# State products in two runs of three units, with output pieces on both sides, in an attention block followed by a gated feed-forward layer

## The chip, the cores and the metric

The kernel runs on one core of a Trainium2 chip. The metric is the device time of one execution in microseconds (us), lower is better. A time is the median of several executions of the same program.

## What is computed

There are 8 batches of 8 heads; each has 512 tokens `x` and 32 state rows, 64 wide. Tokens attend to the state and the state attends to the tokens ("recurrent read"), both through the same scores:

```
xread = softmax(scale * x @ state^T) @ state        # 512 rows a head and batch
sread = softmax(scale * state @ x^T) @ x            #  32 rows a head and batch
y     = heads of [xread; sread] side by side        # (8 * 544) x 512
out   = (relu(y @ w_gate) * (y @ w_val)) @ w_out    # 512 -> 1536 -> 512
```

The kernel never forms `xread`. It multiplies the state with the two weights first, `U = state @ w` (the **state products**), so that `xread @ w` becomes attention weights times `U`. For the 32 state rows a batch it forms `sread` itself.

## The kernel before

**Stages.** The work of a batch is cut into 12 slots, one for each 128 columns of the 1536 hidden features. A slot `(b, jf)` holds four matmuls of `gv` (gate and value, line 314), a ReLU of the gate on ScalarE (`relu`, L338), the product with the value on VectorE (`mult`, L342) and one **output piece** (`out_piece`, four matmuls at L351 with `w_out`) for a tile of hidden features made 18 slots earlier (`lag`). Every third piece closes an output tile: `fin_x` copies it out on ScalarE (L359) and SyncE sends it to memory.

**Order.** The schedule is written out by hand. A literal program covers batches 0 and 1 and the start of batch 2; from slot (2, 4) on a loop emits one slot after the other, and the dictionary `units` adds extra work at the end of a slot (`at(b, jf, f, ...)`). Each engine runs its instructions in the order in which the code emits them.

**Extra work in the loop.** For batch `b` (3 to 7) the slots of batch `b - 1` carry: two halves of the scores with their softmax (`att_half`: matmuls L198, exponential on ScalarE L205, sum, reciprocal and scaling on VectorE L211, L213, L217), the state products (`u_block`), the recurrent read (`sr`) and the transposition of its result (`sr_T`). Slot (2, 10) also holds `state_prep`, which transposes the state of batches 4 to 7 on TensorE (L127) and copies it out on ScalarE (L131).

A **unit** of state products (`u_unit`, L289) is eight matmuls of tile size 64 rows by 32 columns, which share the array, and fills two PSUM banks; `u_out` (L299) casts each bank into `U`. There are six units a batch: gate and value for three stretches of 512 columns. `u_block` emits two units:

```
def u_block(b, lo, engs=("act", "act", "dve", "dve")):
    for w in range(2):
        u_unit(b, w, lo)
        for kc in range(NK):
            u_out(b, w, lo, kc, engs[2 * w + kc])
```

so ScalarE casts both banks of the first unit and VectorE both banks of the second. The blocks stand in slots 7, 9 and 11.

`sr_mm` (L262) is 32 matmuls with 32 columns of weights each; `sr_norm` on VectorE (L269, L271) writes the tile `sn`; `sr_T` (L275) is one TensorE transposition of `sn`, copied into `br` on ScalarE (L276). `x_pad` (L254, GpSimd) fills the other operand of `sr_mm`, two batches ahead in the same buffer, so it waits for the `sr_mm` that used that buffer last. `x_next` (L140, GpSimd) casts the tokens of the next batch.

**Banks.** Of eight PSUM banks six rotate (`"r"`): each request takes the next in turn, whoever asks. `gv` takes two, a unit two, a half of the scores one, `sr_mm` one, `sr_T` one, `state_T` one. The other two (`"o"`) alternate as output accumulators. A matmul into a bank waits until the last reader of that bank is done.

Of the kernel before, what the change touches and what calls it, by code (L numbers as in the profile page):

```python
# [16 lines left out]
def kernel(  # L17
# [17 lines left out]
    NF = d_ff // 128  # L35
# [19 lines left out]
    NK = 2  # L55
# [7 lines left out]
    NX, DP = 2, 66  # L63
# [15 lines left out]
    given, turn = [], {"r": 0, "o": 0}  # L79

    def bank(name, kind="r"):

        if given:
            n = given.pop(0)
        else:
            n = turn["r"] % 6 if kind == "r" else 6 + turn["o"] % 2
            turn[kind] += 1
        return psum.tile([128, 512], FP32, name=name, tag=f"b{n}")

    held = {}  # L90
# [33 lines left out]
    def state_T(g):  # L124
        ps = held["st", g] = bank("stT_ps").bitcast(BF16)[:, 0:512]
        for i in range(4):
            nc.tensor.transpose(ps.rearrange("p (q i m) -> p q i m", i=4, m=8)[:, :, i],  # L127
                                st_b[:, g % 3, i].rearrange("p h d -> p (h d)"), id128)
# [31 lines left out]
    def x_T(b, j):  # L160

        if b not in xT:
            xT_alloc(b)
        ps = bank("xT_ps").bitcast(BF16)[:, 0:512].rearrange("p (c t) -> p c t", c=NC)
        for c in range(NC):
            if b == 0 and j < 2:
                nc.tensor.transpose(ps[:, c], x_head(b)[:, c, 2 * j:2 * j + 2].rearrange("p h d -> p (h d)"), id128)
            else:
                v, h = (x_tail(b), 2 * j - HK) if b == 0 else (xb[b], 2 * j)
                for h2 in range(2):  # L170
                    nc.tensor.transpose(ps[64 * h2:64 * h2 + 64, c], v[:, c, h + h2], id128)
        held["xT", b, j] = ps
# [4 lines left out]
    def x_T2(b, half):  # L177
        if b not in xT:
            xT_alloc(b)
        ps = held["xT2", b, half] = bank("xT_ps").bitcast(BF16).rearrange("p (c j t) -> p c j t", c=NC, j=2)  # L180
        for j in range(2):
            for c in range(NC):
                for h2 in range(2):
                    nc.tensor.transpose(ps[64 * h2:64 * h2 + 64, c, j], xb[b][:, c, 4 * half + 2 * j + h2], id128)
# [68 lines left out]
            src = src.rearrange("p c h d -> p h c d")  # L253
            nc.gpsimd.tensor_copy(out=v[:, hs:hs + src.shape[1]], in_=src)  # L254

    def sr_mm(b):

        ps = held["sr", b] = bank("sr_ps")[:, 0:2 * DP].rearrange("p (r d) -> p r d", r=2)
        for c in range(NC):
            for parity in range(2):  # L260
                for j in range(NJ):
                    nc.tensor.matmul(ps[32 * j:32 * j + 32, parity, 0:D + 1], e_sn[b][:, parity, c, 32 * j:32 * j + 32],  # L262
                                     xa[:, b % NX, H * c + 2 * j + parity, 0:D + 1],
                                     start=(c == 0 and parity == 0), stop=(c == NC - 1), skip_group_check=True)

    def sr_norm(b):
        ps = held["sr", b]
        rr = small.tile([128, 2], FP32, name="rr", tag="rr")
        nc.vector.reciprocal(out=rr, in_=ps[:, :, D])  # L269
        sn = held["sn", b] = small.tile([128, 2, D], BF16, name="sn", tag="sn")  # L270
        nc.vector.tensor_tensor(out=sn, in0=ps[:, :, 0:D], in1=rr.to_broadcast([128, 2, D]), op=ALU.mult)  # L271
# [20 lines left out]
    def u_unit(b, w, lo):  # L292

        u_alloc(b)
        ps = held["u", b, w, lo] = [bank("up"), bank("up")]
        u_mm(ps, b, w, lo, 512)

    def u_out(b, w, lo, kc, eng):
        copy[eng](out=U[b][:, w, kc, lo:lo + 512], in_=held["u", b, w, lo][kc])  # L299
# [17 lines left out]
    def gv(b, jf):  # L317
        if b not in hsb:
            hsb[b] = hpool.tile([128, NF, S], BF16, name="h_sb", tag="h_sb")
        held["gv", b, jf] = [bank("gv_ps"), bank("gv_ps")], hsb[b][:, jf], S  # L320
        for w in range(2):
            for kc in range(NK):
                gv_mm(held["gv", b, jf][0], b, jf, w, kc)

    def gvs(jf):
        f0 = jf * 128
        ps = [bank("gv_ps"), bank("gv_ps")]
        nt = B * Ns
        for w, wsb in ((0, wg_sb), (1, wv_sb)):
            for j in range(NJ):  # L330
                nc.tensor.matmul(ps[w][:, 0:nt], wsb[:, j, f0:f0 + 128], br[:, j].rearrange("p b n -> p (b n)"),  # L331
                                 start=(j == 0), stop=(j == NJ - 1))
        held["gv", B, jf] = ps, hs_sb[:, jf], nt

    def relu(b, jf):
        ps, dst, n = held["gv", b, jf]
        g_sb = held["g", b, jf] = gpool.tile([128, 512], BF16, name="g_sb", tag="g_sb")
        nc.scalar.activation(out=g_sb[:, 0:n], in_=ps[0][:, 0:n], func=AF.Relu)  # L338

    def mult(b, jf):  # L340
        ps, dst, n = held["gv", b, jf]
        nc.vector.tensor_tensor(out=dst, in0=ps[1][:, 0:n], in1=held["g", b, jf][:, 0:n], op=ALU.mult)  # L342
# [4 lines left out]
    def out_mms(src, b, tsub, jfs):  # L347
        if jfs[0] == 0:
            held["o", b, tsub] = o_bank()
        for jf in jfs:  # L350
            nc.tensor.matmul(held["o", b, tsub], src[:, jf, tsub * 128:(tsub + 1) * 128], wo_sb[:, jf],  # L351
                             start=(jf == 0), stop=(jf == NF - 1))
# [4 lines left out]
    def fin_x(b, tsub, eng="act"):  # L357
        o_sb = opool.tile([128, d_model], FP32, name="o_sb", tag="o_sb")
        copy[eng](out=o_sb, in_=held["o", b, tsub])  # L359
        nc.sync.dma_start(out=out_rows(b, tsub), in_=o_sb)  # L360

    def fin_s(t2):
        outr = out.rearrange("(b s) m -> b s m", s=SP)
        o_sb = opool.tile([128, d_model], FP32, name="o_sb", tag="o_sb")
        nc.scalar.copy(out=o_sb, in_=held["o", B, t2])
        for bq in range(4):
            eng = nc.sync if bq % 2 == 0 else nc.scalar
            eng.dma_start(out=outr[t2 * 4 + bq, S:SP], in_=o_sb[bq * Ns:(bq + 1) * Ns])
# [14 lines left out]
    def out_part(b, i):  # L383
        tsub, q = divmod(i, 3)
        out_mms(hsb[b], b, tsub, list(range(4 * q, 4 * q + 4)))

    def out_piece(b, i):
        out_part(b, i)
        if i % 3 == 2:
            fin_x(b, i // 3)  # L390
# [37 lines left out]
    def spin(n, cols=512):  # L428
        for i in range(n):
# [6 lines left out]
             "sc": att_sc, "ex": att_exp, "nr": att_sum, "nx": att_scale, "aT2": att_T2, "ao2": att_out2, "aT": att_T, "ao": att_out,  # L436
             "c": c_unit, "co": c_out, "u": u_unit, "uo": u_out, "gv": gv, "re": relu, "mu": mult, "o": out_part,
             "of": fin_x, "xn": x_next, "xp": x_pad, "sr": sr_mm, "sn": sr_norm}
    program = """
    dx.1.0.2 dx.1.1.2 stc.0.0.act stc.0.1.dve spin.7 stT.0@0 xc.0.0.dve dw.0.0.128 sto.0.act dw.1.0.128 on xc.0.1.dve  # L440
# [31 lines left out]
        assert not given  # L472


    units = {}

    def at(b, jf, f, *args):
        units.setdefault(NF * b + jf, []).append(lambda: f(*args))

    def u_block(b, lo, engs=("act", "act", "dve", "dve")):  # L480
        for w in range(2):
            u_unit(b, w, lo)
            for kc in range(NK):
                u_out(b, w, lo, kc, engs[2 * w + kc])

    def att_half(b, kc):
        att_up(b, kc)
# [7 lines left out]
        att_scale(b, kc)  # L495

    def sr(b):
        sr_mm(b)
        sr_norm(b)

    def state_prep(lo, hi):
# [4 lines left out]
    first, lag = 2 * NF + 4, 18  # L506
    at(2, 4, x_dma, 4, (nc.sync,))
    at(2, 10, state_prep, 4, B)
    for b in range(3, B):
        s, late = b - 1, 2 if b == 3 else 0  # L510
        for i, jf in enumerate((3, 5)):
            at(s, jf + late, att_half, b, i)
        for i, jf in enumerate((7, 9, 11)):
            at(s, jf, u_block, b, 512 * i)
        if b + 1 < B:
            at(s, 9, x_next, b + 1)
            at(s, 9, x_pad, b + 1)
        if b + 2 < B:
            at(s, 10, x_dma, b + 2, (nc.sync,))
    for b in range(B):  # L520
        s, jf = {0: (2, 2), 1: (2, 3), 2: (2, 8), 3: (2, 11)}.get(b, (b - 1, 9))
        if b > 1:
            at(s, jf, sr, b)
        at(*divmod(NF * s + jf + 2, NF), sr_T, b, "act")
    for g in range(first, NF * (B + 1)):
        b, jf = divmod(g, NF)
        gv(b, jf) if b < B else gvs(jf)
        relu(b, jf)
        mult(b, jf)
        if g >= lag:  # L530
            out_piece(*divmod(g - lag, NF))
        for f in units.get(g, ()):
            f()
    for t2 in range(2):
        out_mms(hs_sb, B, t2, list(range(NF)))
        fin_s(t2)
# [33 lines left out]
```

The softmax here doesn't subtract the row's maximum and nothing guards it: scores larger than these inputs give would overflow.

## Time and profile before

| | |
|---|---|
| median of 13 runs | 226.47 us (226.0 to 227.14) |
| profiled execution: time / span | 227.01 us / 225.2 us |
| TensorE busy | 217.8 us (97%) |
| VectorE busy | 129.0 us (57%) |
| ScalarE busy | 124.9 us (55%) |
| GpSimd busy | 53.4 us (24%) |
| granted TensorE clock | full in every slice |

PE is TensorE's matmuls, PEld its weight loads, DVE VectorE, ACT ScalarE, POOL GpSimd, SP SyncE; L289 is line 289 of the kernel. A timeline line reads: start in us, length in us, engine, line, operation, result<-operands, shape and count, and in brackets the idle time before it with what ended it. Lengths of pipelined matmuls overlap: what a group cost TensorE is the distance from its start to the next start. A step of four wide matmuls takes 0.86 us in this measure.

### The profile page before, as it was taken

The page shows a single profiled execution, that of the slowest core. Times are in us where ns is not written, and L with a number is a line of the kernel's source. Part 1 is how long each engine was busy: PE and PEld are TensorE (multiplying, and loading weights), DVE is VectorE, ACT ScalarE, POOL GpSimd, SP SyncE. Part 2 cuts the span into 40 slices and gives each one's busy share as a digit, 9 for nine tenths or more (in the row PEclk, how much of TensorE's full clock was granted, in tenths as well). Part 3 has the DMA queues.
Part 4 walks back from the last instruction along what each step waited for, and adds up shares of the span by engine and source line. Part 5 has one row for each costly group of instructions (what it writes and reads, how often), then busy time and mean ns, then how long its engine had stood idle before and what let it go on. Part 6 is the DMA issues. An engine that isn't in the chain of part 4 may idle for free.

```text
span 225.2 us, 4840 instructions
## 1 busy us (share of the span) xinstructions
PE 217.8 (97%) x1936; PEld 104.9 (47%) x1967; DVE 129.0 (57%) x226; ACT 124.9 (55%) x236; POOL 53.4 (24%) x58
## 2 busy tenths in 40 slices
PE   7999999999999999999999999999999999999994
PEld 3544454444544444444434443444444445666543
DVE  3687888576496657754866467656865443222100
ACT  4699877773556655665566455555556444322221
POOL 8798756502343240006000600000000000000000
PEclk9999999999999999999999999999999999999999
DMA  6999999160809612691149213611311111112132
GB/s 148 179 195 197 207 233 285 35 170 0 249 33 204 220 47 62 144 262 51 48 110 248 89 61 65 131 49 47 93 49 47 48 47 49 48 52 78 60 93 93
DMA packets 37799, 25.48 MB, mean 113 GB/s; under 512 B 18864, under 2 KB 33200, under 8 KB 37776
## 3 DMA queue, kind: packets, MB, share of 16 engines
q1 hardware_dynamic: 24912, 16.85, 26.5%
q0 software_dynamic: 11968, 7.47, 21.5%
q10 hardware_dynamic: 896, 0.85, 1.4%
q8 instruction: 15, 0.25, 0.4%
q14 instruction: 8, 0.07, 0.1%
HBM read 18.35 MB, written 8.91 MB: 121 GB/s over the span
## 4 chain that ended last, share of the span: by engine, by line
PE 89%; DMA 4%; POOL 3%; issue 1%; DVE 1%; ACT 1%; DVEq 0%; POOLq 0%
PE o_ps L351 38%; PE gv_ps L314 36%; PE gv_ps L331 5%; PE up L289 4%; DMA wv_sb<-in_moe_w_val_dram 4%; PE sr_ps L262 1%; PE upc L289 1%; PE o_ps L377 1%; PE sc_ps L198 1%; POOL wg_sb L108 1%; POOL xb L418 1%; POOL wv_sb L108 1%; ACT U L309 1%; DVE h_sb L342 1%; PE aT_ps L233 0%
## 5 line engine op out<-in xcount | busy, mean ns | idle before, releaser
L314 PE MATMUL gv_ps<-ans,U 128*128 128x512 bf16 x367 | 95.0, 380 | 0.9 <-DVE h_sb L342 0.2
L351 PE MATMUL o_ps<-wo_sb,h_sb 128*128 128x512 bf16 x361 | 93.3, 379 | 1.0 <-issue 0.3
L342 DVE TENSOR_TENSOR h_sb<-gv_ps,g_sb 128x512 bf16<-128x512 f32 x96 | 65.3, 688 | 41.8 <-ACT g_sb L338 40.5
L338 ACT ACTIVATE g_sb<-gv_ps 128x512 bf16<-128x512 f32 (+1 forms) x108 | 63.1, 584 | 47.1 <-PE gv_ps L314 32.3
L351 PEld LDWEIGHTS <-h_sb 128*128 128x128 bf16 x372 | 36.0, 98 | 41.0 <-issue 0.7
L314 PEld LDWEIGHTS <-U 128*128 128x128 bf16 x384 | 34.9, 98 | 41.5 <-issue 4.3
L359 ACT COPY o_sb<-o_ps 128x512 f32<-128x512 f32 x29 | 17.0, 585 | 21.1 <-PE o_ps L351 21.1
L299 DVE CAST U<-up 128x512 bf16<-128x512 f32 x36 | 23.2, 685 | 5.6 <-PE up L289 5.6
L299 ACT CAST U<-up 128x512 bf16<-128x512 f32 x36 | 19.4, 593 | 10.1 <-PE up L289 10.1
L140 POOL CAST xb<-xf 128x1024 bf16<-128x1024 f32 x10 | 10.6, 1086 | 53.1 <-DMA xf<-in_x_dram 53.1
L254 POOL COPY xa<-xb 128x2048 bf16<-128x2048 bf16 (+1 forms) x9 | 15.3, 1711 | 14.6 <-PE sr_ps L262 7.4
L211 DVE TENSOR_REDUCE cs<-e_sn 128x16 f32<-128x512 bf16 x16 | 10.9, 683 | 8.1 <-ACT e_sn L205 8.1
L342 DVE TENSOR_TENSOR hs_sb<-gv_ps,g_sb 128x256 bf16<-128x256 f32 x12 | 5.1, 424 | 15.4 <-PE gv_ps L331 10.5
L205 ACT ACTIVATE e_sn<-sc_ps 128x512 bf16<-128x512 f32 x16 | 9.6, 600 | 5.6 <-PE sc_ps L198 5.5
L309 ACT CAST U<-upc 128x512 bf16<-128x512 f32 (+1 forms) x20 | 9.7, 532 | 1.6 <-PE upc L289 1.5
L289 PEld LDWEIGHTS <-stT 64*32 64x32 bf16 x512 | 5.0, 90 | 11.8 <-issue 11.4
L217 DVE TENSOR_TENSOR a_sn<-e_sn,rc 128x512 bf16<-128x512 bf16 x12 | 9.0, 753 | 0.6
L430 PE MATMUL warm_ps<-hs_sb 128*128 128x512 bf16 x20 | 7.0, 461 | 1.4 <-DVE hs_sb L394 1.2
L198 PEld LDWEIGHTS <-xT 128*128 128x128 bf16 x128 | 5.7, 98 | 3.8 <-ACT xT L175 0.7
L331 PE MATMUL gv_ps<-br,wg_sb 128*128 128x256 bf16 x48 | 7.2, 273 | 0.1
L331 PE MATMUL gv_ps<-br,wv_sb 128*128 128x256 bf16 x48 | 7.2, 273 | 0.0
L289 PE MATMUL up<-wg_sb,stT 64*32 64x512 bf16 x144 | 7.2, 386 | 0.0
(64 smaller groups left out, 128.8 us busy)
## 6 DMA issues: line engine op xcount, KB each, us to landing
out_dram<-o_sb SPq DMA_DIRECT2D x31, 256.0 KB, 2.3
xf<-in_x_dram SPq DMA_DIRECT2D x4, 1024.0 KB, 6.2
wo_sb<-in_moe_w_out_dram POOLq DMA_DIRECT2D x2, 768.0 KB, 14.5
wg_sb<-in_moe_w_gate_dram POOLq DMA_DIRECT2D x5, 256.0 KB, 9.0
wv_sb<-in_moe_w_val_dram POOLq DMA_DIRECT2D x5, 256.0 KB, 9.6
xf<-in_x_dram POOLq DMA_DIRECT2D x1, 1024.0 KB, 15.1
xb<-in_x_dram POOLq DMA_DIRECT2D x3, 256.0 KB, 6.5
xb<-in_x_dram POOLq DMA_DIRECT2D x1, 512.0 KB, 11.8
```

Of the source, the lines that this page charges most:

```text
L140: copy[eng](out=xb[b][:, :, hs].rearrange("p c h d -> p h c d"), in_=xf[b][:, hs])
L211: nc.vector.reduce_sum(out=cs, in_=e_v, axis=AX.X)
L254: nc.gpsimd.tensor_copy(out=v[:, hs:hs + src.shape[1]], in_=src)
L289: nc.tensor.matmul(dst[parity][32 * j:32 * j + 32], stT[r:r + 64, b, j, 32 * parity:32 * parity + 32], wsb[r:r + 64, j, lo:lo + n], start= ...
L299: copy[eng](out=U[b][:, w, kc, lo:lo + 512], in_=held["u", b, w, lo][kc])
L309: copy[eng](out=U[b][:, :, kc, lo:lo + n], in_=held["c", b, lo][kc])
L314: nc.tensor.matmul(ps[w], U[b][:, w, kc, f0:f0 + 128], ANS[b][:, kc].rearrange("p c t -> p (c t)"), start=(kc == 0), stop=(kc == NK - 1))
L331: nc.tensor.matmul(ps[w][:, 0:nt], wsb[:, j, f0:f0 + 128], br[:, j].rearrange("p b n -> p (b n)"), start=(j == 0), stop=(j == NJ - 1))
L338: nc.scalar.activation(out=g_sb[:, 0:n], in_=ps[0][:, 0:n], func=AF.Relu)
L342: nc.vector.tensor_tensor(out=dst, in0=ps[1][:, 0:n], in1=held["g", b, jf][:, 0:n], op=ALU.mult)
L351: nc.tensor.matmul(held["o", b, tsub], src[:, jf, tsub * 128:(tsub + 1) * 128], wo_sb[:, jf], start=(jf == 0), stop=(jf == NF - 1))
L359: copy[eng](out=o_sb, in_=held["o", b, tsub])
```

## The change

Per batch 3 to 7 the six units are emitted as **two runs of three** in slots 7 and 10, where there were three runs of two in slots 7, 9 and 11. In each unit ScalarE now casts the first bank and VectorE the second. A slot with a run gets a second output piece after the extra work, so a run has an output piece on both sides; the slot after it then has no piece (`piece <= g - lag`). The recurrent read moves into the slot of a run and follows the run's matmuls: slot 7 for batch 2 (was 8), slot 10 of the batch before for batch 3 (was 11) and for batches 4 to 7 (was 9). Its matmuls write the output bank that is not in use (`"spare"`, which does not advance the turn) instead of a rotating bank. The transposition `sr_T` stands one slot after the recurrent read instead of two: (2, 8) for batch 2 (was (2, 10)), (2, 11) for batch 3 (was (3, 1)), and slot 11 as before for batches 4 to 7. For batches 0 and 1 nothing moves. No operation is added or removed.

```
@@ bank
         if given:
             n = given.pop(0)
+        elif kind == "spare":
+            n = 6 + turn["o"] % 2
         else:
             n = turn["r"] % 6 if kind == "r" else 6 + turn["o"] % 2
             turn[kind] += 1
@@ sr_mm
-    def sr_mm(b):
-        ps = held["sr", b] = bank("sr_ps")[:, 0:2 * DP]...
+    def sr_mm(b, kind="r"):
+        ps = held["sr", b] = bank("sr_ps", kind)[:, 0:2 * DP]...
@@ u_block
-    def u_block(b, lo, engs=("act", "act", "dve", "dve")):
-        for w in range(2):
+    def u_block(b, part):
+        for w, lo in ((0, 0), (1, 0), (0, 512), (1, 512), (0, 1024), (1, 1024))[3 * part:3 * part + 3]:
             u_unit(b, w, lo)
-            for kc in range(NK):
-                u_out(b, w, lo, kc, engs[2 * w + kc])
+            u_out(b, w, lo, 0, "act")
+            u_out(b, w, lo, 1, "dve")
@@ sr
-        sr_mm(b)
+        sr_mm(b, "spare")
         sr_norm(b)
@@ slots
-        for i, jf in enumerate((7, 9, 11)):
-            at(s, jf, u_block, b, 512 * i)
+        for part, jf in enumerate((7, 10)):
+            at(s, jf, u_block, b, part)
+            paired.add(NF * s + jf)
...
-        s, jf = {0: (2, 2), 1: (2, 3), 2: (2, 8), 3: (2, 11)}.get(b, (b - 1, 9))
+        s, jf = {0: (2, 3), 1: (2, 4), 2: (2, 7)}.get(b, (b - 1, 10))
         if b > 1:
             at(s, jf, sr, b)
-        at(*divmod(NF * s + jf + 2, NF), sr_T, b, "act")
+        at(s, jf + 1, sr_T, b, "act")
+    piece = first - lag
     for g in range(first, NF * (B + 1)):
...
-        if g >= lag:
-            out_piece(*divmod(g - lag, NF))
+        if piece <= g - lag:
+            out_piece(*divmod(piece, NF))
+            piece += 1
         for f in units.get(g, ()):
             f()
+        if g in paired:
+            out_piece(*divmod(piece, NF))
+            piece += 1
```

More of the change, by code (lines that the diff above doesn't have):

```diff
@@ L254, in x_pad @@
             nc.gpsimd.tensor_copy(out=v[:, hs:hs + src.shape[1]], in_=src)
-    def sr_mm(b):
-        ps = held["sr", b] = bank("sr_ps")[:, 0:2 * DP].rearrange("p (r d) -> p r d", r=2)
+    def sr_mm(b, kind="r"):
+        ps = held["sr", b] = bank("sr_ps", kind)[:, 0:2 * DP].rearrange("p (r d) -> p r d", r=2)
         for c in range(NC):
@@ L472 @@
         assert not given
-    units = {}
+    units, paired = {}, set()
     def at(b, jf, f, *args):
         units.setdefault(NF * b + jf, []).append(lambda: f(*args))
-    def u_block(b, lo, engs=("act", "act", "dve", "dve")):
-        for w in range(2):
+    def u_block(b, part):
+        for w, lo in ((0, 0), (1, 0), (0, 512), (1, 512), (0, 1024), (1, 1024))[3 * part:3 * part + 3]:
             u_unit(b, w, lo)
-            for kc in range(NK):
-                u_out(b, w, lo, kc, engs[2 * w + kc])
+            u_out(b, w, lo, 0, "act")
+            u_out(b, w, lo, 1, "dve")
     def att_half(b, kc):
```

## The prediction

> **What bounds the kernel now.** I read the page first (busy time, then the chain that ended last), then the groups, then the timeline of one steady batch and of batch 2. From the page:
>
> ```profile
> PE 217.8 (97%) x1936; PEld 104.9 (47%) x1967; DVE 129.0 (57%) x226; ACT 124.9 (55%) x236; POOL 53.4 (24%) x58
> ...
> PE 89%; DMA 4%; POOL 3%; issue 1%; DVE 1%; ACT 1%; DVEq 0%; POOLq 0%
> ...
> L289 PEld LDWEIGHTS <-stT 64*32 64x32 bf16 x512 | 5.0, 90 | 11.8 <-issue 11.4
> ```
>
> TensorE is the bound: 97% busy and 89% of the chain. So the change is worth what it does to the TensorE stream, in which every matmul stays. The third line hints at what it aims at: before weights of the small 64x32 tiles the load side stands 11.4 us in all. That is not the loss itself. The loss is read from starts in the timeline of batch 3 (TensorE only):
>
> ```profile
> 88.20 1.03 PE L351 MATMUL o_ps<-wo_sb,h_sb 128*128 128x512 bf16 x4
> 89.16 0.41 PE L289 MATMUL up<-wg_sb,stT 64*32 64x512 bf16 x8
> 89.39 0.40 PE L289 MATMUL up<-wv_sb,stT 64*32 64x512 bf16 x8
> 89.72 1.04 PE L314 MATMUL gv_ps<-ans,U 128*128 128x512 bf16 x4
> ...
> 93.50 0.40 PE L289 MATMUL up<-wv_sb,stT 64*32 64x512 bf16 x8
> 93.83 0.43 PE L262 MATMUL sr_ps<-xa,e_sn 128*32 128x65 bf16 x32
> 94.19 1.04 PE L314 MATMUL gv_ps<-ans,U 128*128 128x512 bf16 x3
> ```
>
> A piece costs 0.86 from start to start (95.07 to 95.93 in the same view), so the run could start at 89.06 and starts at 89.16: 0.10 to enter. Unit to unit is 0.22. The second unit is followed after 0.33: 0.11 to leave. A run costs **0.21 us** beyond its matmuls. Beside a recurrent read the 0.11 is paid between the two (93.50 to 93.83), and the read itself (0.36) leads into `gv` without a gap. A read on its own pays 0.10 to enter (66.03 + 0.86 = 66.89, start 66.99 below).
>
> Batch 2 is different. It has the second half of the scores and a block in the same slot 7 (chain and timeline around it):
>
> ```profile
> 62.34 2.48 POOL L140 CAST xb<-xf 128x1024 bf16<-128x1024 f32 x2 [3.70 <-DMA xf<-in_x_dram]
> 62.49 1.43 DVE L217 TENSOR_TENSOR a_sn<-e_sn,rc 128x512 bf16<-128x512 bf16 x1
> 63.84 1.27 DVE L342 TENSOR_TENSOR h_sb<-gv_ps,g_sb 128x512 bf16<-128x512 f32 x2
> 64.10 0.41 PE L289 MATMUL up<-wg_sb,stT 64*32 64x512 bf16 x8
> 64.58 0.41 PE L289 MATMUL up<-wv_sb,stT 64*32 64x512 bf16 x8
> 65.04 0.67 DVE L211 TENSOR_REDUCE cs<-e_sn 128x16 f32<-128x512 bf16 x1
> 65.17 1.02 PE L314 MATMUL gv_ps<-ans,U 128*128 128x512 bf16 x3 [0.19 <-DVE h_sb L342]
> 66.03 0.69 DVE L217 TENSOR_TENSOR a_sn<-e_sn,rc 128x512 bf16<-128x512 bf16 x1
> 66.64 1.28 DVE L299 CAST U<-up 128x512 bf16<-128x512 f32 x2
> 66.99 0.31 PEld L262 LDWEIGHTS <-e_sn 128*32 128x32 bf16 x32 [0.42 <-issue]
> 67.59 1.90 POOL L254 COPY xa<-xb 128x2048 bf16<-128x2048 bf16 x1 [2.77 <-PE sr_ps L262]
> 68.63 0.29 DVE L271 TENSOR_TENSOR sn<-sr_ps,rr 128x128 bf16<-128x128 f32 x1
> ```
>
> Here VectorE is behind: its casts of the block start at 66.64, two microseconds after the matmuls, and `sn` is written only at 68.9. Today nobody needs `sn` soon: the transposition stands two slots after the read.
>
> **What the Trainium skill says.** "TensorE: Matmul & The Clock Gate", Part 3, "The mechanism": a weight load overlaps matmuls in flight only where its row group differs, and matmuls start and end strictly in program order. The trace agrees with the first as far as it shows it: 0.10 exposed where the tile shape changes, none between units. The second is what makes a late `sn` costly: `gv` matmuls behind the transposition cannot pass it. "SBUF — State Buffer", section "SBUF: two separate sides": VectorE (also when it reads two SBUF tensors, against a GpSimd operation that reads SBUF) and GpSimd share a port pair as an exclusive lock, the first holds it for its whole instruction. The trace fits: the scaling at 62.49 took 1.43 beside a GpSimd cast that began at 62.34, and 0.69 elsewhere.
>
> **The change part by part.**
>
> *One run less a batch.* Batches 3 to 6 (for `b` = 4 to 7): 4 x 0.21 = -0.84. Batch 2 (for `b` = 3): three runs and a lone read become two runs, -0.21 - 0.10 = -0.31. Ceiling of the gain: -1.15.
>
> *Output pieces moved.* Same number, same order, same banks. `fin_x` and its SyncE transfers come at most a slot sooner, in the same SyncE order; nothing on TensorE waits for them. GpSimd keeps its order too; only `x_pad` follows the moved read. 0. The price if this cover went is a ScalarE copy, 0.58, ahead of a ReLU.
>
> *Six banks in a row, steady batches.* With `gv(7)` ahead, the third unit needs `gv(7)`'s value bank. From batch 3: third unit due at 89.39 + 0.22 = 89.61; the pair of products there starts at 88.32 and ends at 89.60, and a release takes about 0.06 (65.11 to 65.17 above). Stall about 0.06 in slot 7. In slot 10 no scores precede, the product is done 0.3 before. After the run the extra piece (0.86) covers the casts: counted from the run's start, ScalarE casts at 0.48, 1.02, 1.55 (0.54 apart), VectorE at 0.48, 1.08, 1.68 (0.60 apart); the next `gv` starts at 0.65 + 0.11 + 0.86 = 1.62 and needs the first unit's banks, free at 1.02 and about 1.15. Free; without the piece it would stall 0.4. Bounds: 0 to 0.2 each; taken 4 x 0.06 = +0.24.
>
> *Transposition one slot after the read, steady batches.* From the start of the run in slot 10: leave 0.76, read to 1.12, piece to 1.98, `gv(11)` to 2.85, and there is no piece in slot 11, so the transposition is due at 2.85. VectorE: three casts from 0.48 to 2.29, reciprocal (0.19 to the next start), `sn` from 2.48 to 2.77, seen at 2.83. Just in time, but its weight load (0.10) can no longer be pulled ahead: about 0.07 each, bounds 0 to 0.25; 4 x 0.07 = +0.28. In before the same transposition in slot 11 had `sn` two microseconds early.
>
> *Batch 2, slots 7 and 8.* Up to 64.58 as before. Third unit due at 64.80, needs `gv(7)`'s value bank, released at 65.17: late by 0.37, where before the next `gv` lost 0.26 on the same bank. Leave: 65.50; read to 65.86; piece to 66.72; `gv(8)` gate; its value half (due 67.15) needs the first unit's VectorE bank, whose cast runs from 66.64 to 67.3: late by 0.2; end 67.78. Now the transposition of `sn`. VectorE's casts are three now: 66.64, 67.24, 67.85; reciprocal 68.45; `sn` 68.64 to 68.93; transposition at 69.0: **late by 1.2**, with `gv(9)` queued behind it, and ScalarE and VectorE in turn waiting for `gv(9)`. `gv(9)` starts at 69.06, before at 67.36. Of these 1.70, one unit (0.22) and the transposition (0.06) are work done earlier: **+1.42**. The lone read's 0.10 is already in it.
>
> *Batch 2, slots 9 to 11.* One run less, -0.21. `state_prep` stands ahead of the run in slot 10, takes two banks, and the third unit comes round to these; ScalarE's copies of it end 1.49 after its matmuls' start (71.48; copies 71.90, 1.07 for two), the third unit is due 0.66 + 0.10 + 0.44 = 1.20 after: +0.35 with the release. Together +0.14; bounds -0.2 to +0.4. By then `sn` of batch 3 is in time, by 0.4.
>
> Sum: batch 2 1.42 + 0.14 = +1.56; batches 3 to 6 -0.84 + 0.24 + 0.28 = -0.32. Total **+1.24**. Against the profiled execution (227.01, span 225.2) that is 228.25; that execution lies 0.54 above the median of 226.47, so against the median 227.7.
>
> **The rivals.**
>
> *Forecast, 0.68:* as above. With the bounds (batch 2 +1.1 to +2.1, the rest -0.84 to +0.2) 226.9 to 228.7.
>
> *GpSimd gets the port first, 0.12.* `x_pad` now follows a read that starts at 65.50, by the same 0.60 as in before (66.99 to 67.59): 66.10. VectorE's scaling starts at 66.03. If it loses these 0.07, it waits for the 1.90 copy, and casts, `sn` and transposition move by about 1.95: 229.7. For it: a margin of 0.07. Against: both ends follow the same product (65.11), so the margin should hold.
>
> *The waits do not come, 0.10: faster.* If VectorE has `sn` of batch 2 by 67.8 and the product of slot 7 a little earlier, only the saved switches are left: -1.15, 225.3. It decides at 1.1 us: so much must VectorE's chain from exponential to `sn` be shorter than its parts (reduce, reciprocal, scale, three casts, two small ones) measure. Against it: each part is in the trace, and the exponential (64.20 to 64.80) sets the start of the reduction.
>
> *Half of it, 0.10.* The stall in slot 8 comes to about 0.4 and the steady gain is whole: about no change, 226.4.
>
> **How the numbers follow.** A measurement of this kernel can tell about 0.2%, 0.45 us, from no change. Likeliest 227.7. The forecast's range reaches up to the port rival, 229.7, and down towards the no-change case, 226.2; the faster case stays out. Slower is nearly all of the forecast and the port rival, 0.78; same 0.11; faster 0.11.
>
> **What would show it.** In the changed trace: two runs a batch with 0.21 beyond their matmuls; in slot 8 of batch 2 an idle TensorE of about 1.2 ended by `sn`; the third unit late by 0.06 in slot 7, by 0.35 in slot 10 of batch 2; transpositions in slot 11 with gaps below 0.1; batches 3 to 6 shorter by about 0.08 each. Wrong would be: a steady batch longer than before, `sn` of batch 2 on time, or the scaling at 66.03 taking about 2 us.

## The result, and the profile after

The changed kernel takes **229.55 us** in the median of 11 runs (227.89 to 231.05), the kernel before 226.86 beside it (48 runs). The ratio is 1.0128 with a 95% interval of 1.0108 to 1.0148: slower by 2.7 us, where +1.24 was forecast. The sign is as forecast, and so is the place, batch 2; the size is not. The profiled execution took 229.55 with a span of 227.7.

The page of the changed kernel, its lines moved down by two:

```profile
PE 216.2 (95%) x1937; PEld 106.4 (47%) x1967; DVE 130.2 (57%) x226; ACT 124.8 (55%) x236; POOL 53.4 (23%) x58
...
PE 86%; DMA 4%; POOL 3%; DVE 3%; issue 2%; ACT 1%; POOLq 0%; DVEq 0%
...
L219 DVE TENSOR_TENSOR a_sn<-e_sn,rc 128x512 bf16<-128x512 bf16 x12 | 10.0, 833 | 0.6
```

TensorE does the same work in a longer span, and VectorE's share of the chain rises from 1% to 3%. The last line gives the lead: the mean of the twelve softmax scalings was 753 ns in the kernel before and is now 833, 0.96 us more in all. By the timelines two of the twelve changed: the one of slot 5 takes 0.69 where it took 1.43, the one of slot 7 takes 2.38 where it took 0.69. What TensorE waits for in batch 2 (table of waits, window 60 to 80; total, times, longest):

```profile
PE gv_ps L316 <- DVE U L301: 1.9, 1, 1.9
PE srT_ps L277 <- DVE sn L273: 1.0, 1, 1.0
```

And the chain that ended last through slots 7 and 8 of batch 2 (start, length, what):

```profile
64.86 0.60 ACT e_sn L207
...
65.48 0.70 DVE cs L213
...
66.49 2.38 DVE a_sn L219
68.87 1.79 DVE U L301 x3
...
70.78 0.30 DVE sn L273
...
71.13 0.23 PE srT_ps L277
```

For six microseconds the chain is not TensorE's. The scaling takes 2.38 in place of 0.69; the three casts and `sn` follow it, and the transposition ends the stretch. The timeline says why the scaling takes so long:

```profile
65.50 0.10 PEld L291 LDWEIGHTS <-stT 64*32 64x32 bf16 x6 [0.33 <-issue]
...
65.84 0.43 PE L264 MATMUL sr_ps<-xa,e_sn 128*32 128x65 bf16 x32
...
66.44 1.90 POOL L256 COPY xa<-xb 128x2048 bf16<-128x2048 bf16 x1 [0.72 <-PE sr_ps L264]
66.49 2.38 DVE L219 TENSOR_TENSOR a_sn<-e_sn,rc 128x512 bf16<-128x512 bf16 x1
...
68.80 1.87 DVE L301 CAST U<-up 128x512 bf16<-128x512 f32 x3
...
69.53 0.59 PE L316 MATMUL gv_ps<-ans,U 128*128 128x512 bf16 x2 [1.85 <-DVE U L301]
...
71.13 0.23 PE L277 MATMUL srT_ps<-id,sn 128*128 128x128 bf16 x1 [1.01 <-DVE sn L273]
```

GpSimd's pad copy, released by the moved read, begins 0.05 us ahead of the scaling. It ends at 68.34, and the scaling ends 0.53 after that. This is the port rival of the prediction, which had a chance of 0.12. The first line shows what set the time of the read: the weight loads of the third unit stop for 0.33 and go on at 65.50, just after the exponential ends (65.46). Going round the six banks, `gv(7)` takes two, the half of the scores one and the first two units four, so the third unit gets the value bank of `gv(7)` and then the bank of the scores, which the exponential reads. The prediction named only the first of these.

**The bill by stage, from the two traces.** The exponential of slot 7 starts at 64.86 after and 64.20 before; up to there the two programs are the same, and the exponential of slot 5 shows the same distance (61.36 and 60.71), so this 0.66 is the start of the two executions and not the change. `gv` of slot (3, 0) starts at 78.69 after and at 74.72 before: 3.97, less 0.66, less 0.06 for the transposition of batch 3 that is already done: batch 2 loses **3.25**. From then on `sn` comes every 23.42 (101.68, 125.10, 148.52, 171.94) where it came every 23.77 (95.36, 119.13, 142.89, 166.66): batches 3 to 6 gain **0.35 each, 1.4 in all**. 3.25 - 1.4 + 0.66 is 2.5, the difference of the spans. Forecast were +1.56 and -0.32. So both parts were misjudged, in opposite directions.

### The profile page after: what moved, and what is told of

It reads as the page before. It is cut to its first block, busy times and chain, and to the rows that moved or that the text cites. A ratio compares the mean times of both kernels' runs of the same rounds, so it can differ in the third digit from the quotient of the medians.

```text
span 227.7 us, 4841 instructions
## 1 busy us (share of the span) xinstructions
PE 216.2 (95%) x1937; PEld 106.4 (47%) x1967; DVE 130.2 (57%) x226; ACT 124.8 (55%) x236; POOL 53.4 (23%) x58
## 4 chain that ended last, share of the span: by engine, by line
PE 86%; DMA 4%; POOL 3%; DVE 3%; issue 2%; ACT 1%; POOLq 0%; DVEq 0%
PE o_ps L353 37%; PE gv_ps L316 35%; PE gv_ps L333 5%; DMA wv_sb<-in_moe_w_val_dram 4%; PE up L291 4%; PE upc L291 1%; PE sc_ps L200 1%; PE o_ps L379 1%; PE sr_ps L264 1%; DVE a_sn L219 1%; POOL wg_sb L110 1%; DVE U L301 1%; POOL xb L420 1%; POOL wv_sb L110 1%; ACT U L311 1%
## 5 line engine op out<-in xcount | busy, mean ns | idle before, releaser
L353 PE MATMUL o_ps<-wo_sb,h_sb 128*128 128x512 bf16 x357 | 91.6, 379 | 2.1 <-issue 1.9
L316 PEld LDWEIGHTS <-U 128*128 128x128 bf16 x384 | 35.8, 98 | 42.8 <-issue 2.7
L353 PEld LDWEIGHTS <-h_sb 128*128 128x128 bf16 x372 | 35.2, 98 | 39.9 <-issue 1.7
L301 ACT CAST U<-up 128x512 bf16<-128x512 f32 x36 | 18.9, 597 | 9.3 <-PE up L291 9.3
L291 PEld LDWEIGHTS <-stT 64*32 64x32 bf16 x512 | 5.9, 90 | 12.0 <-issue 10.2
L219 DVE TENSOR_TENSOR a_sn<-e_sn,rc 128x512 bf16<-128x512 bf16 x12 | 10.0, 833 | 0.6
L291 PE MATMUL up<-wv_sb,stT 64*32 64x512 bf16 x144 | 7.4, 380 | 0.1
```

The lines of the kernel that those rows point to most:

```text
L219: {"dve": nc.vector, "pool": nc.gpsimd}[eng].tensor_tensor(out=by_pair(a_sn[b], jp).rearrange("p r (j n) -> p r j n", n=Ns), in0=e_v, in1= ...
L291: nc.tensor.matmul(dst[parity][32 * j:32 * j + 32], stT[r:r + 64, b, j, 32 * parity:32 * parity + 32], wsb[r:r + 64, j, lo:lo + n], start= ...
L316: nc.tensor.matmul(ps[w], U[b][:, w, kc, f0:f0 + 128], ANS[b][:, kc].rearrange("p c t -> p (c t)"), start=(kc == 0), stop=(kc == NK - 1))
```

## The experiments

All edits are against the changed kernel unless said otherwise.

**1. Batch 2 as before, the rest changed.**

```
-        sr_mm(b, "spare")
+        sr_mm(b, "spare" if b > 3 else "r")
...
+        if b == 3:
+            for i, jf in enumerate((7, 9, 11)):
+                at(s, jf, u_block2, b, 512 * i)          # the old block of two units
-        for part, jf in enumerate((7, 10)):
+        for part, jf in enumerate((7, 10) if b > 3 else ()):
...
-        s, jf = {0: (2, 3), 1: (2, 4), 2: (2, 7)}.get(b, (b - 1, 10))
+        s, jf = {0: (2, 3), 1: (2, 4), 2: (2, 8), 3: (2, 11)}.get(b, (b - 1, 10))
...
-        at(s, jf + 1, sr_T, b, "act")
+        at(*divmod(NF * s + jf + (2 if b in (2, 3) else 1), NF), sr_T, b, "act")
```

> Slots of batch 2 (work for batch 3, reads of batches 2 and 3) as in the kernel before, the two runs only in batches 3 to 6. Theory (steady batches gain 0.35 us each: 0.21 for the run saved and 0.17 for a bank wait of gv in slot 0 that goes, less small waits; all the loss sits in batch 2): 4 x 0.35 = 1.4 less than before, about 225.4 us beside 226.9. Rival (the steady gain is 0.08 each as forecast, and the shorter period in the trace is an accident of that execution): 0.3 less, 226.5.

Measured: 225.70 against 227.16, ratio 0.9922 (0.9894 to 0.9949), so 1.46 less. The steady gain of 1.4 is real (in the trace `sn` comes every 23.42 here too), and all the loss lies in batch 2. This version beats both kernels.

**2. Only batch 2 changed,** by the same edit with the conditions turned round.

> Only the slots of batch 2 changed (two runs for batch 3, reads of batches 2 and 3 beside them), batches 3 to 6 as before. Theory: the whole loss of batch 2 as in the changed kernel's trace, +3.3 us, about 230.2, in some executions 1 to 1.5 more where the granted TensorE clock falls after the idle stretch. Rival (the forecast's +1.56 for batch 2, the rest of the loss lies elsewhere): 228.4.

Measured: 229.08 against 227.16, ratio 1.0112 (1.0064 to 1.0161). Neither number fits, and the single executions say why: four lie from 228.86 to 229.16, two at 231.31 and 232.10. The traced one is of the first kind (228.86), and there VectorE has the port first (no trace shows the other kind):

```profile
66.12 0.69 DVE L219 TENSOR_TENSOR a_sn<-e_sn,rc 128x512 bf16<-128x512 bf16 x1
66.19 0.81 PE L353 MATMUL o_ps<-wo_sb,h_sb 128*128 128x512 bf16 x3 [0.16 <-issue]
66.19 2.37 POOL L256 COPY xa<-xb 128x2048 bf16<-128x2048 bf16 x1 [1.29 <-PE sr_ps L264]
```

Now the scaling takes 0.69 and the copy is drawn out from 1.90 to 2.37. Such executions lose about 1.8, near the forecast's 1.56. The spread within one kernel is the question that the next experiments take up.

**3. The pad copy taken away from the scaling.** The pads of batches 4 to 7 change buffers, so that the copy for batch 4 waits for the read of batch 3 (slot 10) instead of that of batch 2 (slot 7).

```
+    def pad_of(b):
+        return (b + (b > 3)) % NX
-        v = xa[:, b % NX]...                             # and the same in sr_mm
+        v = xa[:, pad_of(b)]...
-            at(s, 9, x_pad, b + 1)
+            at(s, 11 if b == 3 else 9, x_pad, b + 1)
```

> The changed kernel with GpSimd's pad copy for batch 4 writing the other of its two buffers, so that it waits for the recurrent read of batch 3 instead of batch 2 and comes some 10 us later. Theory (GpSimd's copy takes the shared port 0.05 us ahead of VectorE's scaling in slot 7 and holds it 1.7 us too long): the scaling takes 0.69 instead of 2.38, batch 2 costs the forecast's +1.56, and with -1.4 from the other batches the time is about 227.0, clock full in all executions. Rival (VectorE is late for its own work, the port is not the cause): 229.5 as the changed kernel, scaling still over 2 us.

Measured: 227.49 against 227.16, ratio 1.0011 (0.9997 to 1.0025), 14 runs, all between 227.0 and 227.72. The scaling:

```profile
66.01 0.69 DVE L219 TENSOR_TENSOR a_sn<-e_sn,rc 128x512 bf16<-128x512 bf16 x1
...
68.61 0.29 DVE L276 TENSOR_TENSOR sn<-sr_ps,rr 128x128 bf16<-128x128 f32 x1
...
68.96 0.23 PE L280 MATMUL srT_ps<-id,sn 128*128 128x128 bf16 x1 [1.01 <-DVE sn L276]
```

Another buffer for the copy, and with it another read to wait for, moves the median from 229.55 to 227.49 and removes the spread. In this trace VectorE would have had the port first in the changed kernel too: its exponential and its product stand as in the execution of 227.46 under experiment 8. So the trace alone does not show the effect of the edit; the 14 times do, of which none reaches 228, where 17 of 21 of the changed kernel lie above 228.5 (12 beside the kernel before and nine in experiment 8). The port is the cause of what lies beyond the low group. What stays is the forecast's own mechanism: `sn` at 68.61 (forecast 68.64), transposition at 68.96 (forecast 69.0), a wait of 1.0 (forecast 1.2). With the 1.46 of the other batches, batch 2 costs 0.33 + 1.46 = 1.8 here.

That is more than the forecast's 1.56, and slot 10 shows the rest:

```profile
72.47 0.61 PE L129 MATMUL stT_ps<-id,st_b 128*128 128x128 bf16 x8
72.90 1.07 ACT L133 COPY stT<-stT_ps 128x512 bf16<-128x512 bf16 x2 [0.92 <-PE stT_ps L129]
...
73.24 0.40 PE L294 MATMUL up<-wg_sb,stT 64*32 64x512 bf16 x8
...
73.54 0.90 PE L294 MATMUL up<-wv_sb,stT 64*32 64x512 bf16 x8
...
74.03 0.11 PEld L294 LDWEIGHTS <-stT 64*32 64x32 bf16 x6 [0.40 <-issue]
...
74.36 0.43 PE L267 MATMUL sr_ps<-xa,e_sn 128*32 128x65 bf16 x32
```

The third unit is due at 73.46, 0.22 after the second. Its loads stop after the first bank and go on at 74.03, when ScalarE's second copy of `state_prep` has ended (73.97), so it is 0.57 late.

**4. Experiment 3, and the transposition of batch 2's read two slots later.**

```
-        at(s, jf + 1, sr_T, b, "act")
+        at(s, jf + (3 if b == 2 else 1), sr_T, b, "act")
```

> As the run with the pad in the other buffer, and the transposition of batch 2's recurrent read in slot 10 (three slots after the read) instead of slot 8. Theory: the 1.2 us that TensorE waits for sn in slot 8 go, about 225.8. Rival (the wait only moves to gv(8) or gv(9), whose banks VectorE casts late): less than 0.4 gained, 226.6 or more.

Measured: 227.07 against 227.16, ratio 0.9992 (0.9972 to 1.0011): 0.4 less than experiment 3, not 1.2, so the rival is nearer. By the traces 0.94 is saved from `gv(8)` to the piece behind `gv(9)`, 0.06 of it the transposition itself, and 0.31 is lost again in slot 10. Of the wait for `sn` a part only moves. `gv(8)` and `gv(9)` now stand together, and eight matmuls that take 1.73 elsewhere take 2.22 (66.50 to the piece at 68.72). About 0.2 of this is the value half of `gv(8)`, which waits for VectorE's first cast; the prediction had that. The other 0.3 is `sn` again: the recurrent read wrote the spare output bank, and the piece behind `gv(9)` opens the next output tile in that bank, so it waits until `sn` has been taken out of it:

```profile
68.37 0.29 DVE L276 TENSOR_TENSOR sn<-sr_ps,rr 128x128 bf16<-128x128 f32 x1
...
68.72 0.55 PEld L356 LDWEIGHTS <-h_sb 128*128 128x128 bf16 x4 [0.64 <-DVE sn L276]
68.72 1.04 PE L356 MATMUL o_ps<-wo_sb,h_sb 128*128 128x512 bf16 x4
...
72.38 0.89 PE L294 MATMUL up<-wv_sb,stT 64*32 64x512 bf16 x8
...
73.36 0.22 PE L280 MATMUL srT_ps<-id,sn 128*128 128x128 bf16 x1
...
73.51 0.43 PE L267 MATMUL sr_ps<-xa,e_sn 128*32 128x65 bf16 x32
```

In slot 10 the transposition lands between a run and a read. From the third unit to the read are 1.13 there, where experiment 3 has 0.82 (73.54 to 74.36); between wide matmuls a transposition takes 0.06.

**5. The kernel before, with the transposition ahead of the block of slot 11.** This asks where the 0.35 a batch comes from, of which saved switches explain 0.21.

```
+        if b > 3:
+            at(s, 11, sr_T, b, "act")                    # ahead of u_block in the same slot
         for i, jf in enumerate((7, 9, 11)):
             at(s, jf, u_block, b, 512 * i)
...
-        at(*divmod(NF * s + jf + 2, NF), sr_T, b, "act")
+        if b <= 3:
+            at(*divmod(NF * s + jf + 2, NF), sr_T, b, "act")
```

> The kernel before with one edit: in slot 11 of batches 3 to 6 the transposition of the recurrent read stands ahead of the block of state products instead of behind it, so that the banks go round differently and gv of slot 0 no longer takes the first unit's bank while ScalarE casts it. Theory (half of the steady gain is this wait, 0.17 us a batch, and not the saved tile switches): 4 x 0.17 = 0.7 less than before. Rival (all 0.35 a batch come from the saved run): no change.

Measured: 226.41 against 227.11, ratio 0.9956 (0.9936 to 0.9977), 0.7 less, as the theory has it. The wait was in the kernel before, and the prediction had not seen it. Its timeline around slot (5, 0):

```profile
121.74 0.40 PE L289 MATMUL up<-wv_sb,stT 64*32 64x512 bf16 x8
...
122.10 1.08 ACT L299 CAST U<-up 128x512 bf16<-128x512 f32 x2
122.14 1.20 PE L314 MATMUL gv_ps<-ans,U 128*128 128x512 bf16 x4
...
122.75 0.10 PEld L314 LDWEIGHTS <-U 128*128 128x128 bf16 x1 [0.29 <-issue]
...
123.18 1.03 PE L351 MATMUL o_ps<-wo_sb,h_sb 128*128 128x512 bf16 x4
```

From `gv` at 122.14 to the piece at 123.18 are 1.04, not 0.86. Six banks go round: `gv(11)` two, the block four, the transposition one, so the value half of the next `gv` gets the first bank of the block while ScalarE still casts it (122.10 to about 122.64). The idle load side, 0.29 "issue", is all that shows. With the transposition ahead the same step takes 0.91 (the value half then gets the bank of the transposition), and `sn` comes every 23.62 instead of 23.77: 0.15 a batch by the trace, 0.6 in all.

**6. Batch 3's runs later.** Slots (2, 9) and (3, 0), the reads beside them, the transpositions two slots after.

```
-        for part, jf in enumerate((7, 10)):
-            at(s, jf, u_block, b, part)
-            paired.add(NF * s + jf)
+        for part, g in enumerate((NF * s + 9, NF * s + 12) if b == 3 else (NF * s + 7, NF * s + 10)):
+            at(0, g, u_block, b, part)
+            paired.add(g)
...
-            at(s, 9, x_pad, b + 1)
+            at(s, 11 if b == 3 else 9, x_pad, b + 1)
...
-        s, jf = {0: (2, 3), 1: (2, 4), 2: (2, 7)}.get(b, (b - 1, 10))
+        s, jf = {0: (2, 3), 1: (2, 4), 2: (2, 9), 3: (3, 0)}.get(b, (b - 1, 10))
...
-        at(s, jf + 1, sr_T, b, "act")
+        at(s, jf + (2 if b in (2, 3) else 1), sr_T, b, "act")
```

> The changed kernel with batch 3's two runs in slots (2, 9) and (3, 0), after the scores of that batch, the reads of batches 2 and 3 beside these, the transpositions two slots after, and the pad copy of batch 4 emitted in slot (2, 11). Theory (batch 2 loses because run and read meet VectorE's softmax work in slot 7): VectorE has caught up by slot 9, the two saved switches of batch 2 (0.3) come on top of the 1.4 of the other batches, 1.7 less than before. Rival (batch 2 loses in any place, since six banks and state_prep do not fit together): not below the run that leaves batch 2 as it was.

Measured: 225.70 against 227.11, ratio 0.9918 (0.9892 to 0.9944). Batch 2 can have two runs without a loss, in slots where VectorE is not busy with the softmax: the wait for `sn` and the long scaling are gone. That they bring the 0.3 of two saved switches is not shown by the times: the median is that of experiment 1. The traced execution is faster there: from the exponential of slot 7 to the run in slot 7 of batch 3 it takes 24.22 (64.69 to 88.91), against 24.98 in experiment 1 (64.73 to 89.71) and 24.96 before (64.20 to 89.16). With six executions of each, 0.9 and 1.1 apart among themselves, it stays open, and so does the rival in its own terms (not below experiment 1).

**7. No piece behind a run.** Experiment 1 without its line `paired.add(NF * s + jf)`.

> The kernel with batch 2 as before and two runs in batches 3 to 6, but without the second output piece behind a run (each piece stays in its own slot). Theory (the piece covers the casts): gv behind the run of slot 7 is due 0.76 after the run's start and its second bank is free at about 1.2, so 0.4 a batch in slot 7 and about 0.1 in slot 10 behind the read: 4 x 0.5 = 2.0 more than with the pieces, 0.5 more than before. Rival (the casts are quick enough without): as with the pieces, 1.4 less than before.

Measured: 226.86 against 227.11, ratio 0.9986 (0.9971 to 1.0001), 1.2 more than experiment 1 and hardly less than before: between the two expectations, nearer to the theory. The piece does cover the casts, but is worth 0.3 a batch rather than 0.5 (`sn` comes every 23.68 instead of 23.42). After slot 7 `gv` waits for ScalarE's first cast and not for VectorE's:

```profile
90.21 0.45 PE L291 MATMUL up<-wg_sb,stT 64*32 64x512 bf16 x8
...
90.87 1.02 PE L316 MATMUL gv_ps<-ans,U 128*128 128x512 bf16 x3 [0.21 <-ACT U L301]
```

**8. The changed kernel again,** for the spread of its times: nine executions, one of them traced, and three single traced ones.

> The changed kernel unchanged, for another look at what differs between its executions (227.9 to 231.1). Theory (which engine takes the shared port first decides, and the granted clock falls after the longer idle stretch): an execution near 228 has a scaling of 0.69 in slot 7, one near 229.5 a scaling over 2 with a full clock, one near 231 the same with a clock below 1 for some us after slot 8. Rival (the spread has to do with the start of the program): the scaling is the same in all.

> The changed kernel unchanged, one more execution with its trace. Theory: near 227.6 the scaling of slot 7 takes 0.69, near 229.3 over 2 with a full clock, near 231 over 2 with a granted clock below 1 in the stretch after the idle time of slot 8. Rival: a time near 231 with a full clock everywhere, then a third wait that the other traces do not have.

> A second look of the same kind: 227.6 with a scaling of 0.69, 229.3 with one over 2 and a full clock, 231 with one over 2 and a granted clock below 1 after slot 8; the rival has 231 with a full clock and a third wait.

> A third look of the same kind: 227.6 with a scaling of 0.69, 229.3 with one over 2 and a full clock, 231 with one over 2 and a granted clock below 1 after slot 8; the rival has 231 with a full clock and a third wait.

Measured: a median of 229.13 for the nine (227.32 to 231.02), and 228.98, 227.46, 230.79 and 227.34 for the traced executions. All four fit the theory. They fall into the three groups in which nearly all its executions lie: near 227.5, near 229.2 and near 230.9. The execution of 227.46 (timeline):

```profile
62.38 2.48 POOL L142 CAST xb<-xf 128x1024 bf16<-128x1024 f32 x2 [3.72 <-DMA xf<-in_x_dram]
62.51 1.45 DVE L219 TENSOR_TENSOR a_sn<-e_sn,rc 128x512 bf16<-128x512 bf16 x1
...
66.07 0.69 DVE L219 TENSOR_TENSOR a_sn<-e_sn,rc 128x512 bf16<-128x512 bf16 x1
66.15 2.37 POOL L256 COPY xa<-xb 128x2048 bf16<-128x2048 bf16 x1 [1.29 <-PE sr_ps L264]
```

The execution of 230.79, its timeline and then its table of stages (stretch, its length, TensorE busy and instructions, granted clock, DMA share, GB/s):

```profile
62.69 0.69 DVE L219 TENSOR_TENSOR a_sn<-e_sn,rc 128x512 bf16<-128x512 bf16 x1
...
62.93 2.34 POOL L142 CAST xb<-xf 128x1024 bf16<-128x1024 f32 x2 [4.09 <-DMA xf<-in_x_dram]
...
65.99 1.90 POOL L256 COPY xa<-xb 128x2048 bf16<-128x2048 bf16 x1 [0.72 <-PE sr_ps L264]
66.04 2.39 DVE L219 TENSOR_TENSOR a_sn<-e_sn,rc 128x512 bf16<-128x512 bf16 x1
```

```profile
68.00:70.00 2.00, 0.59 (x2) 1.00 0.15 29
70.00:72.00 2.00, 1.32 (x5) 0.74 1.07 245
72.00:74.00 2.00, 2.00 (x7) 0.50 1.15 213
74.00:76.00 2.00, 2.00 (x11) 0.91 0.88 268
```

There are two races for the port, and in all five traces of the changed kernel the first decides the second. In slot 5 GpSimd's cast of the next tokens, released when they arrive (62.38, 62.93), meets the first scaling (62.51, 62.69). If the cast comes first, the first scaling is held up and the product of slot 7 is late; then both sides of the second race follow that product (the read through the value bank of `gv(7)`), and VectorE wins it by 0.08. If the scaling wins, the product is in time, both sides follow the exponential of slot 7 (the read through the bank of the scores), and GpSimd wins by 0.05. An early win is paid back later with interest. This is read from the traces; no edit here fixes the first race. Nor is it shown what sets the time at which the tokens arrive: experiment 2 is the same program up to there, and by their times, four of its six executions had the cast first, against 4 of 21 of the changed kernel.

The third group is the second with the TensorE clock at half for a few microseconds. The loss in these stretches, (1 - 0.74) x 2 + (1 - 0.50) x 2 + (1 - 0.91) x 2 = 1.7, is the distance from 229.1 to 230.8. All executions agree: the ten of the changed kernel above 230.5 have a mean granted clock of 0.990 to 0.993, the others 0.997 or more. That the waits bring the clock down is argued from the order in time; in experiment 3, which has only the wait of 1.0, no mean clock of its 14 executions is below 0.999.

## Why the prediction was right in its sign and wrong in its size

- *What bounds the kernel, the 0.10 in and 0.11 out of a run.* Right. In the changed kernel batch 3's runs enter at 93.06, 0.09 after the piece ahead of them was due to end, and 99.18, 0.10 after. The saved runs are worth the -0.21 a batch that was set: the 0.35 a batch leave 0.24 for them beside the terms below. One reading was too wide: the prediction says that the trace agrees where a weight load is said to overlap matmuls only if its row group differs. It does not: in the kernel before, the 128x128 weights of the piece at 61.18 begin to load at 60.97, under the 128x128 matmuls of `gv`.
- *Steady batches, -0.32: wrong by 1.1.* Two terms failed. The sum left out that `gv` of slot 0 loses 0.17 a batch in the kernel before; the step "six banks in a row" followed the banks through the new order only and never through the old one. And the transposition a slot after the read was charged +0.07 a batch: `gv(11)` starts at 101.19 and the transposition at 102.05, 0.86 later, so it costs nothing, though its weight load starts only at 102.03:

```profile
101.19 1.03 PE L316 MATMUL gv_ps<-ans,U 128*128 128x512 bf16 x4
...
102.03 0.10 PEld L277 LDWEIGHTS <-sn 128*128 128x128 bf16 x1 [0.31 <-DVE sn L273]
102.05 0.22 PE L277 MATMUL srT_ps<-id,sn 128*128 128x128 bf16 x1
```

  The third unit's 0.06 in slot 7 is there: its weight loads have an idle 0.17, and the run's end comes 0.39 after the last unit's start instead of 0.33. -0.21 - 0.17 + 0.06 is -0.32 a batch, -0.35 was measured.
- *Batch 2, slots 7 and 8, +1.42: right where VectorE has the port.* In experiment 3 `gv(9)` starts at 69.02; forecast was 69.06.
- *Batch 2, slots 9 to 11, +0.14: too small.* In experiment 3 `gv(3, 0)` starts at 76.52, against 74.72 before: 1.80, less the 0.06 of the transposition and 0.02 of start is 1.72. Up to `gv(9)` it is 1.36 (69.02 less 67.36, less 0.02, and less the 0.28 of work done earlier), so 0.36 for these slots. The term that failed is the wait for the copies of `state_prep`: set at 0.35, it is 0.57. The copies end 1.49 after the start of the transposes, as set, but the third unit is due sooner. The prediction counted 0.66 for the eight transposes; the kernel before shows 0.45:

```profile
71.48 0.61 PE L127 MATMUL stT_ps<-id,st_b 128*128 128x128 bf16 x8
...
71.93 0.22 PE L275 MATMUL srT_ps<-id,sn 128*128 128x128 bf16 x1
```

  With 0.45 the unit is due after 0.99 and the sum gives 0.56; less the 0.21 of the saved run that is 0.35.
- *The rival of the port: the mechanism right, its chance wrong.* This is the step that decided the size: the overlap of GpSimd's copy with the scaling was left out of the sum, and it costs batch 2 another 1.5 (3.25 less 1.72). The prediction gave it 0.12 because "both ends follow the same product (65.11), so the margin should hold". Both ends do follow the same event, but which event depends on the first race, since the third unit waits for the bank of the scores as well as for that of the product, and the margin changes sign with it: +0.08 behind the product, -0.05 behind the exponential. The trace of before showed only one outcome of the first race, a scaling at 62.49 behind a cast at 62.34; 0.15 us apart, it was no safer a premise than the 0.07 that I did doubt. It was the common case, 17 of 21 executions. The price, 1.95, was somewhat high: 227.5 to 229.2 is 1.7, and the traces give 1.5.
- *The clock.* Not foreseen. It makes the upper of the three groups.
- *The sum.* With both corrections batch 2 costs 1.8 where VectorE has the port first and 3.3 where GpSimd has it, the rest gains 1.4: +0.4 or +1.9, or +3.6 with the clock down. The three groups, 227.5, 229.2 and 230.9, lie 0.4, 2.1 and 3.8 above the 227.11 of the kernel before in experiment 8, and 0.25 more above the 226.86 of the first comparison. So the right sign is owed to the port: without its loss, in experiment 3, the changed kernel can't be told from the kernel before (1.0011, 0.9997 to 1.0025), because the forecast's two parts err in opposite directions (+1.8 for +1.56, -1.4 for -0.32). That it came out clearly slower is the rival's doing and, for the forecast itself, luck. The range has slips of its own: by the bounds named its lower end is 226.7 and not 226.9 (226.47 + 1.1 - 0.84), and the bounds of the single terms let the steady batches reach +0.96, not +0.2.

## What to carry to other kernels

When an operation is moved, follow what it releases on every engine, and look for pairs of VectorE and GpSimd operations that start within a tenth of a microsecond of each other: here such a pair was a coin, and its price was nearly the other's whole duration (1.69 of 1.90). Ask of each side which event it follows, and whether another such pair upstream changes that event. A bank that is borrowed ties its reader to the bank's next user. Walk the rotation of the banks through the old order as carefully as through the new one, since a stall inside a group of matmuls shows only as a distance between starts that is too long.

## What the runs showed of the hardware

- The Trainium skill, "SBUF — State Buffer", "SBUF: two separate sides", says that the first to start holds the shared port pair for its whole instruction. The traces agree in both directions: a scaling of 0.69 takes 2.38 behind a copy of 1.90 that began 0.05 earlier, and a copy of 1.90 takes 2.37 behind a scaling that began 0.08 earlier.
- The Trainium skill, "TensorE: Matmul & The Clock Gate", Part 1, states a half clock after an idle window of about 3.4 us. The trace agrees on the half (0.50 in one stretch), but TensorE had no idle stretch that long: in the execution of 230.79 the clock fell after two waits of 1.9 and 1.0 with two matmuls between. The executions of 228.98 and 229.55 have the same two waits and a full clock, so the two waits don't always bring it down.
- A transposition whose weights arrive only as the matmul ahead of it ends costs TensorE nothing (0.86 from start to start).
